# Fused LayerNorm and MLP on one core: two tiles of the first block transposed by DMA, a wave of seven rows, one PSUM ring

## The chip, the core and the metric

The kernel runs on one core of a Trainium2 chip. A core has five engines with instruction queues of their own: TensorE (PE, matrix multiplication; its weight loads are shown as PEld), VectorE (DVE), ScalarE (ACT), GpSimd (POOL) and SyncE (SP, which here only issues DMAs and waits for them). They work side by side and wait for one another through semaphores. PE writes its results to PSUM, which has 8 banks of 512 float32 values on each of 128 partitions; all other data lies in SBUF, also on 128 partitions.

The metric is the device time of one execution in microseconds (us). Lower is better.

## What is computed

```python
def _layernorm(x, axis=-1, eps=1e-5):
    m = jnp.mean(x, axis=axis, keepdims=True)
    v = jnp.var(x, axis=axis, keepdims=True)
    return (x - m) / jnp.sqrt(v + eps)

def reference(x, w1, b1, w2, b2):
    y = _layernorm(x, axis=-1)
    h = _gelu(jnp.einsum("bsd,df->bsf", y, w1) + b1)
    return jnp.einsum("bsf,fd->bsd", h, w2) + b2
```

There are 2048 tokens (one batch), D = 1024, F = 3584, all in bfloat16. The gelu is the tanh approximation.

## The kernel before

**Tiling.** The 2048 tokens are 16 tiles of 128 (one token on each partition) and 4 blocks of 4 tiles. For each block the kernel computes the first product transposed: a *row* r of it is 128 of the 3584 hidden features (28 rows), by 512 tokens. The stationary operand is a 128x128 piece of `w1_sb`, the moving one is `yT_sb`, the normalized block with features on the partitions; 8 matmuls over D make a row (`pe_cell`, L337 to L350, the matmul's line is L344). ACT takes the row out of PSUM with bias and gelu into `hT_sb` (`act_gelu`, L354). The second product then takes `hT_sb` as the stationary operand and `w2_sb` as the moving one: 28 matmuls of 512 columns make one half of an output tile (`out_chunk`, L387), which VectorE adds `b2` to and puts into `o_sb` (L398), and SyncE stores (L403).

**LayerNorm and transposes.** VectorE computes mean and variance of a tile (L252, L256), adds eps (L263), GpSimd takes the power -0.5 (L260), and VectorE normalizes in place in `x_sb` (L268, event `y{i}`). Then the tile has to be transposed into `yT_sb`. For blocks 1 to 3 VectorE does this with 32x32 transposes (L300), in the time that it has left. For block 0 TensorE does it, since everything waits for it: `pe_T` (L311) makes eight 128x128 transposes (L316) into the PSUM tile `ps_t`, and ACT copies them to `yT_sb` in two halves (L324, events `te{i}_0` and `te{i}_1`, for the two halves of D in `KGROUPS`).

**The opening wave.** So that PE can start on tile 0 alone, the first `R` = 4 rows of block 0 are computed tile by tile (L424 to L436), each in its own bank, as *cells* of 128 columns. For each tile, the first half of D is done for all four rows, then the transposes of the next tile are put in, then the second half. With the last tile the four rows go to gelu. The remaining rows of block 0 are whole rows of 512 columns (`mm1_rows(0, R)`). Ahead of the wave, PE runs matmuls on a tile of ones (`warm`, L409), and one small transpose for the bias `b1` (L419).

**Loads.** All loads are issued at the start, without waits, three pieces of x by ACT and the rest by SyncE, each queue in order: parts of tiles 0 to 3, `b1`, and w1 in eight chunks. Chunks 0 to 3 are 256 columns wide with half of D each, chunks 4 and 5 have 512 columns (chunk 4: rows 4 to 7, chunk 5: rows 8 to 11), 6 and 7 have 1024. Then come block 1 of x, w2, b2, and the other blocks of x. A matmul waits for the chunk that its row lies in.

**PSUM.** Three pools: `ps_t` (one bank) for the transposes, `ps_1` with `NB1` = 5 banks for rows of the first product, taken in turn by `new_unit`, and `ps_2` with `NB2` = 2 banks for the halves of output tiles. A bank is taken again when its gelu, or its output addition, has been done.

**Order.** Each engine's instructions are put down as a list in program order; waits are on named events. Only on VectorE the order is planned: `crit` (output additions, with the estimated time at which PE is done) and `fill` (LayerNorm and transposes of the next block) are merged by estimated times (L471 to L486). On PE, ACT, SyncE and GpSimd the order is that of the code.

Of the kernel before, what the change touches and what calls it, by code (L numbers as in the profile page):

```python
# [5 lines left out]
ACT = mybir.ActivationFunctionType  # L6
# [5 lines left out]
P = 128  # L12
TB = 512
TPB = TB // P
R_WAVE = 4
K_GROUPS = 2
NB1 = 5
NB2 = 2
NOB = 2
TAIL_PIECES = 4  # L20
WARM_A = ((26, None), (8, "st0_0"), (8, "mv0"), (6, "rstd0"))
# [63 lines left out]
def bass_standalone__mixer_channel_mlp__prompt_kernel(  # L85
# [18 lines left out]
    HC = D // 2  # L104
    assert ST % TB == 0 and D % P == 0 and F % P == 0 and D % NCH == 0
    assert HC <= 512 and DT * P * 2 <= 2048 and FT >= 4 and FT <= P
    R = max(1, min(R_WAVE, FT - 2, NB1 - 1))
    nkg = max(1, min(K_GROUPS, DT))
    KGROUPS = [(h * DT // nkg, (h + 1) * DT // nkg) for h in range(nkg)]
    assert NB1 + NB2 + 1 <= 8  # L110

    w1_chunks = []
    c0 = 0
# [28 lines left out]
    with ExitStack() as es:  # L142
# [18 lines left out]
        vpe_sb = sb("vpe_sb", [P, NT], F32)  # L161
        rstd_sb = sb("rstd_sb", [P, NT], F32)

        ps_t = ps("ps_t", [P, 1, 1024], BF16)
        ps_1 = ps("ps_1", [P, NB1, 512], F32)
        ps_2 = ps("ps_2", [P, NB2, 512], F32)
        ps_2b = ps_2[:, :, :].bitcast(BF16)

        sp = _Prog(None)
        pe = _Prog("s_pe")  # L170
# [140 lines left out]
        def pe_T(i):  # L311
            waits = [f"y{i}", "ident"]
            if last_te[0] is not None:
                waits.append(last_te[0])
            for j in range(DT):
                pe.op(lambda e, i=i, j=j: e.transpose(out=ps_t[:, 0, j * P:(j + 1) * P],  # L316
                                                      in_=x_sb[:, i, j * P:(j + 1) * P], identity=ident[:, :]),
                      waits=waits if j == 0 else (), sig=(f"tp{i}" if j == DT - 1 else None))
            blk, t = divmod(i, TPB)
            evs = []  # L320
            for h, (j0, j1) in enumerate(KGROUPS):
                src = ps_t[:, 0, j0 * P:j1 * P].rearrange("p (j s) -> p j s", j=j1 - j0)
                dst = yT_sb[:, blk % 2, j0:j1, t * P:(t + 1) * P]
                act.op(lambda e, dst=dst, src=src: e.copy(out=dst, in_=src), waits=[f"tp{i}"], sig=f"te{i}_{h}")  # L324
                evs += [f"te{i}_{h}"] * (j1 - j0)
            yT_ev[i] = evs
            last_te[0] = evs[-1]

        unit_n = [0]
        unit_gelu = []  # L330

        def new_unit():
            u = unit_n[0]
            unit_n[0] += 1
            return u % NB1, ([unit_gelu[u - NB1]] if u >= NB1 else [])

        def pe_cell(b, r, t0, t1, bank, waits, sig, dts=None):  # L337
            n0, n1 = t0 * P, t1 * P
            dts = list(range(DT)) if dts is None else list(dts)
            waits = list(waits)  # L340
            for k, dt in enumerate(dts):
                w = (waits if k == 0 else []) + [f"w1c{w1_chunk_of(r, dt)}"]
                w += [yT_ev[b * TPB + t][dt] for t in range(t0, t1)]
                pe.op(lambda e, b=b, r=r, dt=dt, n0=n0, n1=n1, bank=bank: e.matmul(  # L344
                    ps_1[:, bank, n0:n1], lhsT=w1_sb[:, dt, r * P:(r + 1) * P], rhs=yT_sb[:, b % 2, dt, n0:n1],
                    start=(dt == 0), stop=(dt == DT - 1)),
                    waits=w, sig=(sig if dt == DT - 1 else None))
            pe_t[0] += len(dts) * _mm_us(n1 - n0)
            if dts[-1] == DT - 1:
                est[sig] = pe_t[0]  # L350

        def act_gelu(r, t0, t1, bank, wait_ev, sig):
            n0, n1 = t0 * P, t1 * P
            act.op(lambda e, r=r, n0=n0, n1=n1, bank=bank: e.activation(  # L354
                out=hT_sb[:, r, n0:n1], in_=ps_1[:, bank, n0:n1], func=ACT.Gelu_apprx_tanh,
                bias=b1_sb[:, r:r + 1], scale=1.0),
                waits=[wait_ev, "b1c"], sig=sig)
            unit_gelu.append(sig)

        hT_row = {}  # L360

# [5 lines left out]
            hT_row[(b, r)] = f"g_{b}_{r}"  # L367
            mm1_done[b] = sig

        grp_n = [0]  # L370
        grp_oe = []
        crit = []
        fill = []
        store_last = {}

        def out_chunk(b, st, c0, c1, region, prev_store):
            ti = b * TPB + st
            ob = ti % NOB
            g = grp_n[0]
            grp_n[0] += 1  # L380
            bank = g % NB2
            sig = f"m2_{ti}_{c0}"
            waits = [f"w2c{ci}" for ci in range(nw2c)]
            if g >= NB2:
                waits.append(grp_oe[g - NB2])
            for ft in range(FT):
                pe.op(lambda e, st=st, ft=ft, c0=c0, c1=c1, bank=bank: e.matmul(  # L387
                    ps_2[:, bank, 0:c1 - c0], lhsT=hT_sb[:, ft, st * P:(st + 1) * P], rhs=w2_sb[:, ft, c0:c1],
                    start=(ft == 0), stop=(ft == FT - 1)),
                    waits=(waits if ft == 0 else []) + [hT_row[(b, ft)]],  # L390
                    sig=(sig if ft == FT - 1 else None))
            pe_t[0] += FT * _mm_us(c1 - c0)
            est[sig] = pe_t[0]
            dwaits = [sig, "b2"]
            if prev_store is not None:
                dwaits.append(prev_store)
            oe = f"oe_{ti}_{c0}"
            crit.append((est[sig], (lambda e, ob=ob, c0=c0, c1=c1, bank=bank: e.tensor_tensor(  # L398
                out=o_sb[:, ob, c0:c1], in0=ps_2[:, bank, 0:c1 - c0], in1=b2_sb[:, c0:c1], op=ALU.add),
                dwaits, oe, 0.2 + (c1 - c0) * 1e-3), b))  # L400
            grp_oe.append(oe)
            sev = f"st_{ti}_{c0}"
            sp.op(lambda e, ti=ti, ob=ob, c0=c0, c1=c1: e.dma_start(of[ti * P:(ti + 1) * P, c0:c1], o_sb[:, ob, c0:c1]),  # L403
                  waits=[oe], sig=sev, sem=f"d_st_{ob}_{region}", inc=16)
            store_last[(ob, region)] = sev

        def warm(n, gate=None):
            for _ in range(n):
                pe.op(lambda e: e.matmul(ps_2[:, NB2 - 1, 0:P], lhsT=ones[:, :], rhs=ones[:, :],  # L409
                                         start=True, stop=True), waits=["ones"] + ([gate] if gate else []))  # L410

        act.op(lambda e: e.preload_act_table(ACT.Gelu_apprx_tanh))  # L412
# [2 lines left out]
        for o in ln_seq(list(range(TPB))):  # L415
            dve_put(o)

        pe_T(0)
        pe.op(lambda e: e.transpose(out=ps_2b[:, 0, 0:FT], in_=b1r_sb[:, :], identity=ident[0:FT, 0:FT]),  # L419
              waits=["ident", "b1"], sig="b1t")  # L420
        act.op(lambda e: e.copy(out=b1_sb[:, :], in_=ps_2b[:, 0, 0:FT]), waits=["b1t"], sig="b1c")  # L421
        warm(N_WARM_B)
        wave = [new_unit() for _ in range(R)]
        for t in range(TPB):  # L424
            lastt = (t == TPB - 1)
            for h, (j0, j1) in enumerate(KGROUPS):
                for r in range(R):
                    sig = f"m1_0_{r}" if lastt else f"m1_0_{r}_w{t}"
                    pe_cell(0, r, t, t + 1, wave[r][0], wave[r][1] if (t == 0 and h == 0) else [], sig,
                            dts=range(j0, j1))  # L430
                    if lastt and j1 == DT:
                        act_gelu(r, 0, TPB, wave[r][0], sig, f"g_0_{r}")
                        hT_row[(0, r)] = f"g_0_{r}"
                if t + 1 < TPB and h == 0:
                    pe_T(t + 1)
                    pe_t[0] += DT * 0.056  # L436

        def mm1_rows(b, r0):
            for r in range(r0, FT):
                mm1_row(b, r)  # L440

        mm1_rows(0, R)
        for b in range(NB):
            if b + 1 < NB:
                tiles = list(range((b + 1) * TPB, (b + 2) * TPB))
                rel = est[x_ev[tiles[0]][0]]
                for o in ln_seq(tiles):
                    fill.append((rel, o, b + 1))
                rel_t = max(rel, est[mm1_done[b - 1]] if b - 1 in mm1_done else 0.0)
                for i in tiles:  # L450
                    for o in ops_T(i):
                        fill.append((rel_t, o, b + 1))
            if b > 0:
                mm1_rows(b, 0)
            for st in range(TPB):
                for dh in range(DH):
                    c0, c1 = dh * NCH, (dh + 1) * NCH
                    ob = (b * TPB + st) % NOB
                    prev = store_last.get((ob, dh))
                    last = (b == NB - 1 and st == TPB - 1 and dh == DH - 1)  # L460
                    if last and TAIL_PIECES > 1:
                        pw = NCH // TAIL_PIECES
                        for k in range(TAIL_PIECES):
                            out_chunk(b, st, c0 + k * pw, c0 + (k + 1) * pw, dh if k == 0 else f"{dh}p{k}", prev)
                    else:
                        out_chunk(b, st, c0, c1, dh, prev)

        for sev in store_last.values():
            sp.op(None, waits=[sev])
# [74 lines left out]
```

## Time and profile before

| | us |
|---|---|
| median of 3 runs | 400.81 (400.67 to 400.83) |
| span of the profiled execution, first to last instruction | 399.1 |
| PE, matmuls of the first product (L344), busy | 193.9 |
| PE, matmuls of the second product (L387), busy | 193.2 |
| ACT, gelu (L354), busy | 76.7 |
| VectorE, transposes of blocks 1 to 3 (L300), busy | 83.7 |
| PE, transposes of block 0 (L316), 32 in all, busy | 2.5 |

"Busy" is the union of the times in which an instruction of the group runs. The median is 1.7 us more than the span; the profile shows nothing of what lies around the span. The granted TensorE clock is full in all 40 slices of the page. The DMA engines are at 90% or more for the first six slices, some 55 us, while the weights are loaded, and nearly idle afterwards.

Matmuls overlap in the trace: one of 128 columns is shown with 219 ns, but a new one begins every 56 ns. The chain of waits, which follows one piece of work to the next, is what their pace is read from.

### The profile page before, as it was taken

The page shows a single profiled execution, that of the slowest core. Times are in us where ns is not written, and L with a number is a line of the kernel's source. Part 1 is how long each engine was busy: PE and PEld are TensorE (multiplying, and loading weights), DVE is VectorE, ACT ScalarE, POOL GpSimd, SP SyncE. Part 2 cuts the span into 40 slices and gives each one's busy share as a digit, 9 for nine tenths or more (in the row PEclk, how much of TensorE's full clock was granted, in tenths as well). Part 3 has the DMA queues.
Part 4 walks back from the last instruction along what each step waited for, and adds up shares of the span by engine and source line. Part 5 has one row for each costly group of instructions (what it writes and reads, how often), then busy time and mean ns, then how long its engine had stood idle before and what let it go on. Part 6 is the DMA issues. An engine that isn't in the chain of part 4 may idle for free.

```text
span 399.1 us, 4683 instructions
## 1 busy us (share of the span) xinstructions
PE 393.4 (99%) x2026; PEld 189.5 (47%) x2061; DVE 140.1 (35%) x307; ACT 82.3 (21%) x122; POOL 9.5 (2%) x23
## 2 busy tenths in 40 slices
PE   8999999999999999999999999999999999999997
PEld 7844444444444444444444444444444444444446
DVE  6208999889894004988100000001100000001101
ACT  2544330000044332000024334100003334400000
POOL 1102000100001000000000000000000000000000
PEclk9999999999999999999999999999999999999999
DMA  8999930000000000000000000000000000000001
GB/s 262 370 386 387 387 133 15 26 13 29 26 1 2 0 0 2 26 15 26 27 15 0 0 2 0 6 21 26 15 26 13 2 0 0 2 13 26 15 26 28
DMA packets 17614, 23.64 MB, mean 59 GB/s; under 512 B 1466, under 2 KB 10042, under 8 KB 17594
## 3 DMA queue, kind: packets, MB, share of 16 engines
q1 hardware_dynamic: 17162, 22.95, 16.5%
q10 hardware_dynamic: 432, 0.39, 0.3%
q8 instruction: 16, 0.26, 0.3%
q14 instruction: 4, 0.03, 0.0%
HBM read 19.14 MB, written 4.19 MB: 58 GB/s over the span
## 4 chain that ended last, share of the span: by engine, by line
PE 97%; DMA 1%; DVE 1%; issue 1%; POOL 0%; DVEq 0%
PE ps L344 48%; PE ps L387 48%; DMA x_sb<-in_x_dram 1%; PE ps_t L316 1%; DVE st_sb L252 0%; POOL rstd_sb L260 0%; DVE x_sb L268 0%; PE ps L409 0%; DVE o_sb L398 0%; DVE mv_sb L256 0%; DVE vpe_sb L263 0%; PE ps L419 0%; DVEq L72 0%
## 5 line engine op out<-in xcount | busy, mean ns | idle before, releaser
L344 PE MATMUL ps<-yT_sb,w_sb 128*128 128x512 bf16 (+1 forms) x976 | 193.9, 358 | 0.9
L387 PE MATMUL ps<-w_sb,hT_sb 128*128 128x512 bf16 (+1 forms) x961 | 193.2, 360 | 1.0
L344 PEld LDWEIGHTS ps<-yT_sb,w_sb 128*128 128x128 bf16 x992 | 91.8, 98 | 101.9 <-issue 0.2
L387 PEld LDWEIGHTS ps<-w_sb,hT_sb 128*128 128x128 bf16 x980 | 91.3, 98 | 102.6
L354 ACT ACTIVATE hT_sb<-ps,b_sb 128x512 bf16<-128x512 f32 x112 | 76.7, 688 | 257.2 <-PE ps L344 257.2
L300 DVE STREAM_TRANSPOSE yT_sb<-x_sb 32x256 bf16<-32x256 bf16 x192 | 83.7, 436 | 32.5 <-PE ps L344 29.6
L398 DVE TENSOR_TENSOR o_sb<-ps,b_sb 128x512 bf16<-128x512 f32 (+1 forms) x35 | 22.6, 646 | 198.6 <-PE ps L387 198.4
L252 DVE BATCH_NORM_STATS2 st_sb<-x_sb 128x6 f32<-128x512 bf16 x32 | 21.6, 685 | 20.3 <-DMA x_sb<-in_x_dram 20.3
L260 POOL TENSOR_TENSOR rstd_sb<-vpe_sb,nhalf 128x1 f32<-128x1 f32 x16 | 8.8, 550 | 114.6 <-DVE vpe_sb L263 114.6
L268 DVE TENSOR_SCALAR x_sb<-x_sb,mv_sb,rstd_sb 128x1024 bf16<-128x1024 bf16 x16 | 8.7, 547 | 3.4 <-POOL rstd_sb L260 2.7
L409 PE MATMUL ps<-ones 128*128 128x128 bf16 x56 | 5.6, 276 | 1.4 <-POOL ones L245 1.0
L324 ACT COPY yT_sb<-ps_t 128x512 bf16<-128x512 bf16 x8 | 4.3, 589 | 7.3 <-PE ps_t L316 7.3
L409 PEld LDWEIGHTS ps<-ones 128*128 128x128 bf16 x56 | 4.7, 127 | 2.0 <-POOL ones L245 1.0
L256 DVE BATCH_NORM_AGGREGATE mv_sb<-st_sb 128x2 f32<-128x12 f32 x16 | 3.4, 209 | 1.7
L263 DVE TENSOR_SCALAR vpe_sb<-mv_sb 128x1 f32<-128x1 f32 x16 | 2.5, 154 | 0.6
L316 PE MATMUL ps_t<-ident,x_sb 128*128 128x128 bf16 x32 | 2.5, 220 | 0.1
L316 PEld LDWEIGHTS ps_t<-ident,x_sb 128*128 128x128 bf16 x32 | 1.8, 98 | 0.4 <-DVE x_sb L268 0.2
L412 ACT ACT_TABLE_LOAD x1 | 1.3, 1283 | 2.2 <-issue 2.2
L246 POOL TENSOR_SCALAR_AFFINE_SELECT ident<-ones 128x128 bf16<-128x128 bf16 x1 | 0.3, 294 | 0.1
L245 POOL MEMSET ones<- 128x128 bf16 x1 | 0.2, 205 | 0.3 <-POOLq L529 0.3
L421 ACT CAST b_sb<-ps 128x28 f32<-128x28 bf16 x1 | 0.2, 200 | 0.0
L419 PE MATMUL ps<-ident,b1r_sb 28*128 28x28 bf16 x1 | 0.2, 183 | 0.0
(6 smaller groups left out, 0.6 us busy)
## 6 DMA issues: line engine op xcount, KB each, us to landing
w_sb<-in_w_dram SPq DMA_DIRECT2D x4, 1792.0 KB, 18.4
w_sb<-in_w_dram SPq DMA_DIRECT2D x2, 2048.0 KB, 16.2
out_dram<-o_sb SPq DMA_DIRECT2D x31, 128.0 KB, 1.7
x_sb<-in_x_dram SPq DMA_DIRECT2D x3, 1024.0 KB, 14.1
w_sb<-in_w_dram SPq DMA_DIRECT2D x2, 1024.0 KB, 9.0
w_sb<-in_w_dram SPq DMA_DIRECT2D x4, 256.0 KB, 4.7
x_sb<-in_x_dram SPq DMA_DIRECT2D x2, 256.0 KB, 4.3
x_sb<-in_x_dram ACTq DMA_DIRECT2D x3, 128.0 KB, 3.4
```

The costliest lines, as they stand in the source:

```text
L252: return (lambda e, i=i, h=h: e.bn_stats(st_sb[:, i, 6 * h:6 * (h + 1)], x_sb[:, i, h * HC:(h + 1) * HC]), [x_ev[i][h]], f"st{i}_{h}", 0.65)
L256: return (lambda e, i=i: e.bn_aggr(mv_sb[:, i, :], st_sb[:, i, :]), [f"st{i}_0", f"st{i}_1"], f"mv{i}", 0.33)
L260: pool.op(lambda e, i=i: e.tensor_tensor(out=rstd_sb[:, i:i + 1], in0=vpe_sb[:, i:i + 1], in1=nhalf[:, i:i + 1], op=ALU.pow), waits=[f"vpe ...
L268: return (lambda e, i=i: e.tensor_scalar(out=x_sb[:, i, :], in0=x_sb[:, i, :], scalar1=mv_sb[:, i, 0:1], scalar2=rstd_sb[:, i:i + 1], op0= ...
L300: res.append((lambda e, src=src, dst=dst: e.transpose(out=dst, in_=src), waits, (f"tr{i}" if lastop else None), 0.47))
L316: pe.op(lambda e, i=i, j=j: e.transpose(out=ps_t[:, 0, j * P:(j + 1) * P], in_=x_sb[:, i, j * P:(j + 1) * P], identity=ident[:, :]), waits ...
L324: act.op(lambda e, dst=dst, src=src: e.copy(out=dst, in_=src), waits=[f"tp{i}"], sig=f"te{i}_{h}")
L344: pe.op(lambda e, b=b, r=r, dt=dt, n0=n0, n1=n1, bank=bank: e.matmul(ps_1[:, bank, n0:n1], lhsT=w1_sb[:, dt, r * P:(r + 1) * P], rhs=yT_sb ...
L354: act.op(lambda e, r=r, n0=n0, n1=n1, bank=bank: e.activation(out=hT_sb[:, r, n0:n1], in_=ps_1[:, bank, n0:n1], func=ACT.Gelu_apprx_tanh, ...
L387: pe.op(lambda e, st=st, ft=ft, c0=c0, c1=c1, bank=bank: e.matmul(ps_2[:, bank, 0:c1 - c0], lhsT=hT_sb[:, ft, st * P:(st + 1) * P], rhs=w2 ...
L398: crit.append((est[sig], (lambda e, ob=ob, c0=c0, c1=c1, bank=bank: e.tensor_tensor(out=o_sb[:, ob, c0:c1], in0=ps_2[:, bank, 0:c1 - c0], ...
L409: pe.op(lambda e: e.matmul(ps_2[:, NB2 - 1, 0:P], lhsT=ones[:, :], rhs=ones[:, :], start=True, stop=True), waits=["ones"] + ([gate] if gat ...
```

## The change

In block 0, only tiles 0 and 1 are still transposed by `pe_T` (`N_PE_T` = 2). For tiles 2 and 3 ACT issues a DMA that transposes from `x_sb` to `yT_sb` (`act_T`), after the tile has been normalized. The wave has seven rows (`R` + `R_LATE`). PE first does four rows on tiles 0 and 1 as before; then rows 4 to 6 on both tiles together, as 256 columns; then all seven rows on tile 2, and on tile 3, in cells of 128 columns and over the whole of D. After the wave come rows 7 to 27.

The three PSUM pools become one of eight banks, `ps_a`, through which rows and output halves go in turn (`new_unit`, with `bank_free` holding the event that frees a bank). Bank 7 is used for the transposes of tiles 0 and 1 and is the eighth unit, so row 7 waits for the copies of tile 1. The warming matmuls and the small transpose of `b1` write to banks 5 and 6.

On PE, 16 transposes fall away; rows 4 to 6 of block 0 are 24 matmuls of 256 and 48 of 128 columns in place of 24 of 512. On ACT, four copies fall away and two DMAs are added. On VectorE, the plan comes out slightly different: one output addition stands ahead of a normalization instead of behind it, and the transposes around block 0's first output additions are 52, 11 and 1 in place of 53 and 11. The order on SyncE and GpSimd is the same.

```diff
 R_WAVE = 4
+R_LATE = 3
+N_PE_T = 2
-NB1 = 5
-NB2 = 2
+NBANK = 8
+WARM_BANK = 5
+B1_BANK = 6
+T_BANK = 7
...
-        ps_t = ps("ps_t", [P, 1, 1024], BF16)
-        ps_1 = ps("ps_1", [P, NB1, 512], F32)
-        ps_2 = ps("ps_2", [P, NB2, 512], F32)
-        ps_2b = ps_2[:, :, :].bitcast(BF16)
+        ps_a = ps("ps_a", [P, NBANK, 512], F32)
+        ps_ab = ps_a[:, :, :].bitcast(BF16)
...
+        def act_T(i):
+            blk, t = divmod(i, TPB)
+            dst = yT_sb[:, blk % 2, :, t * P:(t + 1) * P]
+            act.op(lambda e, i=i, dst=dst: e.dma_start_transpose(dst, x_sb[:, i, :]), waits=[f"y{i}"], sig=f"dt{i}",
+                   sem=f"d_dt{i}", inc=16)
+            yT_ev[i] = [f"dt{i}"] * DT
...
         def new_unit():
             u = unit_n[0]
             unit_n[0] += 1
-            return u % NB1, ([unit_gelu[u - NB1]] if u >= NB1 else [])
+            bank = u % NBANK
+            return bank, ([bank_free[bank]] if bank in bank_free else [])
...
-        wave = [new_unit() for _ in range(R)]
-        for t in range(TPB):
-            lastt = (t == TPB - 1)
+        wave = [new_unit() for _ in range(RW)]
+        bank_free[T_BANK] = f"te{N_PE_T - 1}_{len(KGROUPS) - 1}"
+        for t in range(N_PE_T):
             for h, (j0, j1) in enumerate(KGROUPS):
                 for r in range(R):
-                    sig = f"m1_0_{r}" if lastt else f"m1_0_{r}_w{t}"
-                    pe_cell(0, r, t, t + 1, wave[r][0], wave[r][1] if (t == 0 and h == 0) else [], sig,
+                    pe_cell(0, r, t, t + 1, wave[r][0], wave[r][1] if (t == 0 and h == 0) else [], f"m1_0_{r}_w{t}",
                             dts=range(j0, j1))
-                    if lastt and j1 == DT:
-                        act_gelu(r, 0, TPB, wave[r][0], sig, f"g_0_{r}")
-                        hT_row[(0, r)] = f"g_0_{r}"
-                if t + 1 < TPB and h == 0:
+                if t + 1 < N_PE_T and h == 0:
                     pe_T(t + 1)
                     pe_t[0] += DT * 0.056
+        for t in range(N_PE_T, TPB):
+            act_T(t)
+        for r in range(R, RW):
+            waits = ["b1c"] if r == B1_BANK else ([])
+            pe_cell(0, r, 0, N_PE_T, wave[r][0], waits, f"m1_0_{r}_w0")
+        for t in range(N_PE_T, TPB):
+            lastt = (t == TPB - 1)
+            for r in range(RW):
+                sig = f"m1_0_{r}" if lastt else f"m1_0_{r}_w{t}"
+                pe_cell(0, r, t, t + 1, wave[r][0], [], sig)
+                if lastt:
+                    act_gelu(r, 0, TPB, wave[r][0], sig, f"g_0_{r}")
+                    hT_row[(0, r)] = f"g_0_{r}"
...
-        mm1_rows(0, R)
+        mm1_rows(0, RW)
```

## The prediction

> **What bounds the kernel now.** I read the page's busy times first, then the chain of waits, then the opening of that chain in order of time. The first lines are from the page.
>
> ```profile
> span 399.1 us, 4683 instructions
> ...
> PE 393.4 (99%) x2026; PEld 189.5 (47%) x2061; DVE 140.1 (35%) x307; ACT 82.3 (21%) x122; POOL 9.5 (2%) x23
> ...
> PE 97%; DMA 1%; DVE 1%; issue 1%; POOL 0%; DVEq 0%
> ```
>
> TensorE (PE) holds 97% of the chain that ends last. So a change counts in two ways only: it takes matmul time off, or it makes PE wait. The stretch that is changed lies in the first 22 us. The chain there (start us, us, engine and line, count) is:
>
> ```profile
> 8.93 0.50 PE ps_t L316 x8
> 9.42 1.79 PE ps L344 x32
> 11.21 0.52 PE ps_t L316 x8
> 11.73 1.79 PE ps L344 x32
> 13.52 0.53 PE ps_t L316 x8
> 14.05 2.68 PE ps L344 x48
> 16.73 0.05 issue
> 16.78 10.74 PE ps L344 x49
> ```
>
> The reader is to see that PE already runs through: transposes of tiles 1, 2, 3 (L316) between cells of the wave (L344), with no DMA or ACT piece among them. Out of it come three prices. A 128-column cell matmul takes 1.79/32 = 0.0559 us. A 512-column one takes (10.74 + 0.05)/49 = 0.2202 us. The two tiles whose transposes go took 0.52 + 0.53 us. Rows 4 to 6 (24 matmuls of 512 columns from 16.78) end at 16.78 + 24 x 0.2202 = 22.07. At that point the same work is done before and after the change: the first product of block 0 for rows 0 to 6. I compare there, and nothing later differs on PE.
>
> Two inputs set what the new order can do. VectorE's timeline has the normalized tiles 1, 2 and 3:
>
> ```profile
> 8.20 0.55 DVE L268 TENSOR_SCALAR x_sb<-x_sb,mv_sb,rstd_sb 128x1024 bf16<-128x1024 bf16 x1
> ...
> 10.51 0.55 DVE L268 TENSOR_SCALAR x_sb<-x_sb,mv_sb,rstd_sb 128x1024 bf16<-128x1024 bf16 x1
> ...
> 12.82 0.55 DVE L268 TENSOR_SCALAR x_sb<-x_sb,mv_sb,rstd_sb 128x1024 bf16<-128x1024 bf16 x1 [0.67 <-POOL rstd_sb L260]
> ```
>
> Tile 2 is ready at 11.06, tile 3 at 13.37. Second, the loads on SyncE's queue. Its timeline gives the issue (start us, us), and the DMA view of that one issue, in the fence after it, the us from issue to landing (last number):
>
> ```profile
> 5.43 0.43 SPq L183 DMA_DIRECT2D w_sb<-in_w_dram  x1
> ```
>
> ```profile
> w_sb<-in_w_dram SPq DMA_DIRECT2D x1, 1024.0 KB, 7.2
> ```
>
> This is w1 chunk 4, the columns of rows 4 to 7: it lands at 5.43 + 7.2 = 12.63. Before, nobody noticed, since row 4 starts at 16.78.
>
> **The change, part by part.** *Removed from PE:* 16 transposes, 0.52 + 0.53 = 1.05 us, all on the chain. Their four ACT copies (589 ns each in the page's groups) go too; ACT had idle time around them, so nothing. *Regrouped:* rows 4 to 6 become 24 matmuls of 256 columns and 48 of 128 columns. No row shows 256 columns; between the two prices per 128 columns (0.0559 and 0.2202/4 = 0.0551) it is 0.110 to 0.112, I take 0.111: 24 x 0.111 = 2.66, and 48 x 0.0559 = 2.68, sum 5.34 against 5.29, so +0.05. The issue gap of 0.05 I leave out on the new side. Were nothing late, the new order would run: 48 cells from 9.42 (tile 0's second half and tile 1) to 12.10, late rows over tiles 0 and 1 to 14.76, then 56 cells of tile 2 (3.13) and 56 of tile 3 (3.13) to 21.02. That is 1.05 us before 22.07.
>
> *New wait 1, weights.* The late rows' first cell needs chunk 4, which lands at 12.63, not 12.10. From a release to the first result the chain needs 0.18 us (tile 1 ready 8.75, first transpose 8.93). So they begin at 12.81: 0.71 us of the 1.05 are gone, the late rows end at 15.47, and the floor for the whole is 15.47 + 6.26 = 21.73, which is -0.34. Behind this wait stands all of PE's queue, that is everything.
>
> *New wait 2, tile 2 by DMA.* ACT's queue now waits for tile 2 after the copies of tile 1 (9.46 + 1.07 = 10.53 in its timeline, so it is there in time), and issues at about 11.11. Behind it on ACT stand the second DMA and the gelus, the first of which is not due before tile 3's cells; they lose nothing. PE wants the tile for 15.47, so 4.2 us from issue are free, and each us more costs one us. *New wait 3, tile 3:* issued at 13.42, wanted at 18.60 less 0.18, so 5.0 us are free. The trace has no DMA transpose. The nearest rows are loads of the same 256 KB tile, those of tiles 2 and 3 on SyncE:
>
> ```profile
> x_sb<-in_x_dram SPq DMA_DIRECT2D x1, 256.0 KB, 3.2
> ```
>
> ```profile
> x_sb<-in_x_dram SPq DMA_DIRECT2D x1, 256.0 KB, 5.4
> ```
>
> The first met short queues, the second stood behind 1 MB of weights in its own queue. The transpose has ACT's queue to itself but meets weights on the same 16 engines (the windows from 8 to 14 us give a full DMA share, at 347 to 352 GB/s). ACT's last 128 KB load, in that position, took 3.4 us; 128 KB more at half of 350 GB/s are 0.75, so I take 3.4 + 0.8 = 4.2. Then tile 2 lands at 15.31, its cells start at 15.49 and the end is 21.75: -0.32. Tile 3 lands at 17.62 and doesn't count. With 3.2 the floor holds (-0.34); with 5.4 tile 2 lands at 16.51, the end is 16.51 + 0.18 + 6.26 = 22.95, +0.88. The far bound is a DMA with as many runs: in the diff its destination is 8 pieces of 128 elements on each of 128 partitions, 1024 pieces, as many as the 1 MB chunks have (8 pieces of 512 on 128 partitions). Those took 7.2 (chunk 4) and 10.8 (chunk 5, the next issue). They are rival 1.
>
> A rule that speaks against the change: the Trainium skill, "VectorE: DVE Perf Modes", section "The three transpose paths", puts one 128x128 block at 390 ns on TensorE and 1309 ns by DMA, and advises TensorE where the result may go to PSUM. The trace has TensorE at 0.5 us for eight blocks, far below eight times 390. Eight DMA blocks one after the other would be an estimated 10.5 us a tile; tile 3 would land near 32 us, and the kernel would need some 414 us. Against that stands "Advanced Engine Details and Errata", section "X-Bar Transpose (TRN2)": transposing DMAs are as fast as others. By this the sum would be the one above. No row here shows either.
>
> *Moved and paid nowhere.* The 0.5 MB of transpose traffic takes about 1.5 us from the loads at 350 GB/s. Chunk 5 (issued 5.91, landing 16.7) is wanted by row 8, after 21.7 + 1.8 = 23.5: 6.8 us of cover. SyncE's order of DMAs stays; POOL's too. *One PSUM ring:* a bank comes back after eight units instead of five (rows) or two (output groups); its release was a gelu (688 ns) or an eviction (646 ns) with at least one unit of 1.76 us between, and PE's whole idle time on these lines is 1.9 us. Nothing is gained or lost; without cover it would cost some 0.7 us a group. VectorE moves one eviction ahead of a normalization and splits its transposes 52 and 12 instead of 53 and 11; those are 0.4 us of an engine with 35% load, whose first block-0 eviction waits for PE. Nothing.
>
> **The sum.** -1.05 + 0.05 - 0.05 + 0.71 + 0.02 = -0.32 us: a span of 398.8 in place of 399.1. The median of the runs, 400.81, is 1.7 above the span; carried over, 400.5 us. What can be told from no change here is about 0.2%, 0.8 us, so this is no change.
>
> **The rivals.** *1, slower: the DMAs move piece by piece.* If 1024 short pieces take turns with the weights' rows, a tile costs what a 1024-row chunk costs. With 7.2 us tile 2 lands at 18.31 and the end is 24.75: +2.7, 403.5 us. With 10.8 for tile 3, which follows in the same queue, 13.42 + 10.8 + 0.18 + 3.13 = 27.5: +5.5, 406.3. It decides from a landing 5.3 us after issue (+0.8). For it: the engines are saturated until 55 us. Against: bytes are a quarter of a chunk's. *2, slower: ACT's issue is held.* SyncE's own issues get stuck once much is queued, as its timeline shows:
>
> ```profile
> 9.92 2.92 SPq L183 DMA_DIRECT2D w_sb<-in_w_dram  x1
> ...
> 12.88 5.43 SPq L183 DMA_DIRECT2D x_sb<-in_x_dram  x1
> ```
>
> If what holds them is shared by both queues, tile 3's DMA starts at 18.36 and lands at 22.56; the end is 25.87: +3.8, 404.6. Against: ACT's three issues took 0.46 us each, but before the queues were full. *3, faster: chunk 4 is in time.* Were its last part early enough, the end would be 21.02: -1.05, 399.8 us. Against: this needs it 0.7 us earlier and tile 2 within 3.5 us, and the new traffic can only delay it.
>
> **How the numbers follow.** Forecast 0.50, of which 0.06 over +0.8 (the 5.4 row); its own range is 400.3 to 401.7. Rival 1 0.22, rival 2 0.18, rival 3 0.08, and 0.02 for smaller losses over 0.8. Faster by over 0.2%: 0.08. Within: 0.44. Slower: 0.06 + 0.22 + 0.18 + 0.02 = 0.48. Losses have more cases, each smaller than the forecast. The range leaves out rival 3 below and rival 1's upper half above: 400.2 to 404.7.
>
> **What would show it.** Right: the chain has a DMA piece of w_sb of about 0.5 us ahead of the 256-column matmuls, both transposes land within 4 to 5 us of issue, and row 7 starts near 21.7 us. Rival 1: the DMA view gives the transposes over 5.3 us and PE's wait names yT_sb. Rival 2: ACT's issue itself lasts us. Rival 3: no piece for w_sb. The forecast is wrong if PE's idle time in the first 25 us exceeds 1.5 us, or if the rest of the kernel no longer runs at 0.2202 us a matmul.

## The result and the profile after

The changed kernel needs 411.56 us (411.50 to 411.68, 4 runs) against 400.82 us of the kernel before in the same session (400.67 to 400.92): a ratio of 1.0266, 95% interval 1.0254 to 1.0278. That is slower by 10.7 us. The profiled execution agrees: a span of 409.9 us in place of 399.1.

The page of the changed kernel, part 4 (the chain that ended last, by engine and by line), has a new entry: the DMA transpose.

```profile
PE 92%; DMA 5%; SPq 1%; DVE 1%; issue 1%; POOL 0%; DVEq 0%
PE ps_a L406 47%; PE ps_a L355 45%; DMA yT_sb<-x_sb 4%; DMA x_sb<-in_x_dram 1%; SPq L186 1%; DVE st_sb L255 0%; DVE x_sb L271 0%; POOL rstd_sb L263 0%; DVE o_sb L391 0%; DVE mv_sb L259 0%; DVE vpe_sb L266 0%; DVEq L76 0%
```

Its timeline in the opening (start us, us, engine, line; in brackets the idle time before and what ended it):

```profile
11.22 8.15 ACTq L335 DMA_TRANSPOSE yT_sb<-x_sb  x2
...
13.04 2.79 PE L355 MATMUL ps_a<-yT_sb,w_sb 128*128 128x256 bf16 x24 [0.80 <-DMA w_sb<-in_w_dram]
...
23.20 5.89 PEld L355 LDWEIGHTS ps_a<-yT_sb,w_sb 128*128 128x128 bf16 x56 [7.65 <-DMA yT_sb<-x_sb]
23.20 6.08 PE L355 MATMUL ps_a<-yT_sb,w_sb 128*128 128x128 bf16 x56 [7.37 <-DMA yT_sb<-x_sb]
```

PE waits 0.8 us for chunk 4, runs the late rows, and then stands still for 7.4 us for tile 2. Then the 56 cells of tile 2 take 6.08 us; those of tile 3 take 3.30 in the chain below. The DMA view of the two transposes, one issue at a time (last number: us from issue to landing):

```profile
yT_sb<-x_sb ACTq DMA_TRANSPOSE x1, 11.9
```

```profile
yT_sb<-x_sb ACTq DMA_TRANSPOSE x1, 15.9
```

Tile 2 lands at 11.22 + 11.9 = 23.1, tile 3 at 13.53 + 15.9 = 29.4. The chain in order of time shows which of them sets the end:

```profile
13.53 15.89 DMA yT_sb<-x_sb
29.42 0.05 issue
29.47 3.30 PE ps_a L355 x56
32.77 0.05 issue
```

Row 7 starts at 32.82 in place of 22.07: 10.75 us later, which is the whole difference of 10.8 us between the spans. From there on the two kernels run alike.

Why the transposes are slow is seen in the DMA view of the changed kernel for 17 to 21 us (queue: packets, MB, share of 16 engines; q1 is SyncE's queue, q10 ACT's):

```profile
q1 hardware_dynamic: 687, 1.41, 90.2%
q10 hardware_dynamic: 683, 0.17, 19.2%
```

Both queues get the same number of packets, not the same bytes. A packet of the weights has 2048 bytes and takes 0.902 x 16 x 4 us / 687 = 84 ns of an engine; one of a transpose has 256 bytes and takes 18 ns. A closer look, from 18.000 to 18.094 us, shows the turns:

```profile
q1 hardware_dynamic: 16, 0.03, 89.4%
q10 hardware_dynamic: 16, 0.00, 19.1%
```

In 94 ns there are 16 packets of each queue. One of the weights fills 84 ns of an engine, so none of the 16 engines can have two: each takes one packet from each queue in turn. The next four such stretches, to 18.47 us, read the same (80 and 80 in all). A tile is 1024 transpose packets, 64 for each engine. By the packets' times it needs 64 x (84 + 18) = 6.5 us while the weights flow; by these turns, in which the packets overlap a little (the shares add up to 109%), 64 x 0.094 = 6.0. Tile 3 landed 6.3 us after tile 2. And for the first 4 us there are no transpose packets at all (same view, 11.2 to 15.2 us):

```profile
q1 hardware_dynamic: 1308, 1.41, 107.9%
q8 instruction: 1, 0.02, 1.8%
```

### The profile page after: what moved, and what is told of

It is laid out like the page before. It is cut to its first block, busy times and chain, and to the rows that moved or that the text cites. A ratio compares the mean times of both kernels' runs of the same rounds, so it can differ in the third digit from the quotient of the medians.

```text
span 409.9 us, 4744 instructions
## 1 busy us (share of the span) xinstructions
PE 395.7 (97%) x2058; PEld 194.0 (47%) x2093; DVE 140.1 (34%) x307; ACT 79.8 (19%) x118; POOL 9.6 (2%) x23
## 3 DMA queue, kind: packets, MB, share of 16 engines
q1 hardware_dynamic: 17162, 22.95, 16.2%
## 4 chain that ended last, share of the span: by engine, by line
PE 92%; DMA 5%; SPq 1%; DVE 1%; issue 1%; POOL 0%; DVEq 0%
PE ps_a L406 47%; PE ps_a L355 45%; DMA yT_sb<-x_sb 4%; DMA x_sb<-in_x_dram 1%; SPq L186 1%; DVE st_sb L255 0%; DVE x_sb L271 0%; POOL rstd_sb L263 0%; DVE o_sb L391 0%; DVE mv_sb L259 0%; DVE vpe_sb L266 0%; DVEq L76 0%
## 5 line engine op out<-in xcount | busy, mean ns | idle before, releaser
L355 PE MATMUL ps_a<-yT_sb,w_sb 128*128 128x512 bf16 (+2 forms) x1021 | 196.9, 354 | 9.5 <-DMA yT_sb<-x_sb 7.6
L406 PE MATMUL ps_a<-w_sb,hT_sb 128*128 128x512 bf16 (+1 forms) x964 | 193.4, 360 | 0.8
L355 PEld LDWEIGHTS ps_a<-yT_sb,w_sb 128*128 128x128 bf16 x1040 | 97.0, 101 | 108.4 <-DMA yT_sb<-x_sb 8.0
L406 PEld LDWEIGHTS ps_a<-w_sb,hT_sb 128*128 128x128 bf16 x980 | 91.3, 98 | 102.6
L365 ACT ACTIVATE hT_sb<-ps_a,b_sb 128x512 bf16<-128x512 f32 x112 | 76.3, 688 | 272.8 <-PE ps_a L355 272.8
L391 DVE TENSOR_TENSOR o_sb<-ps_a,b_sb 128x512 bf16<-128x512 f32 (+1 forms) x35 | 22.6, 646 | 208.4 <-PE ps_a L406 208.3
L255 DVE BATCH_NORM_STATS2 st_sb<-x_sb 128x6 f32<-128x512 bf16 x32 | 21.6, 685 | 21.9 <-DMA x_sb<-in_x_dram 21.8
L417 PE MATMUL ps_a<-ones 128*128 128x128 bf16 x56 | 5.6, 276 | 1.5 <-POOL ones L248 1.0
L417 PEld LDWEIGHTS ps_a<-ones 128*128 128x128 bf16 x56 | 4.7, 127 | 2.1 <-POOL ones L248 1.0
L327 ACT COPY yT_sb<-ps_a 128x512 bf16<-128x512 bf16 x4 | 2.1, 589 | 5.0 <-PE ps_a L319 5.0
L319 PE MATMUL ps_a<-ident,x_sb 128*128 128x128 bf16 x16 | 1.2, 220 | 0.1
```

The source lines that it names most:

```text
L255: return (lambda e, i=i, h=h: e.bn_stats(st_sb[:, i, 6 * h:6 * (h + 1)], x_sb[:, i, h * HC:(h + 1) * HC]), [x_ev[i][h]], f"st{i}_{h}", 0.65)
L417: pe.op(lambda e: e.matmul(ps_a[:, WARM_BANK, 0:P], lhsT=ones[:, :], rhs=ones[:, :], start=True, stop=True), waits=["ones"] + ([gate] if g ...
```

## The experiments

All are edits of the changed kernel. Ratios are against the kernel before, measured in the same session (400.85 to 400.94 us).

**e1_hold_loads.** Are the transposes slow by themselves, or by company?

```diff
+        sp.op(None, waits=[f"dt{TPB - 1}"])
         for ci in range(len(w1_chunks)):
             if ci not in w1_issued:
                 load_w1(ci)
```

> SyncE waits for both transposes before it issues w1 chunk 5 and all later loads, so the transposes meet no weights. Theory A (in the changed kernel each 256-byte packet of a transpose takes turns with one 2048-byte packet of the weights, 84 + 18 ns a pair and engine, 64 pairs a tile): tile 2 lands within 6 us of its issue in place of 11.9, tile 3 within 6 in place of 15.9, and the kernel needs 401 to 403 us. Theory B (the transpose itself is slow, whatever else the engines do): tile 2 again lands about 12 us after issue, tile 3 about 6 us later, and the time stays at 411 to 413. Theory C, on the 4.1 us between issue and the first packet (11.22 to 15.3): if ACT's issue is held up by SyncE's queued loads, the first packet comes 1 to 1.5 us after issue here; if the transpose's own preparation takes it, 4 us stay.

Measured: 401.28 us (400.55 to 401.67), ratio 1.0007 (0.9997 to 1.0016). The DMA view of tile 2's and tile 3's transpose, and the queues from 14 to 16.2 us:

```profile
yT_sb<-x_sb ACTq DMA_TRANSPOSE x1, 4.1
```

```profile
yT_sb<-x_sb ACTq DMA_TRANSPOSE x1, 3.1
```

```profile
q10 hardware_dynamic: 1581, 0.39, 89.4%
```

Alone, the same transposes land in 4.1 and 3.1 us, at 0.39 MB in 2.2 us = 177 GB/s, and the loss is gone. The first packet comes 1.2 us after issue. So theory B falls and A holds. C was still open: both a stuck issue and packets lying ahead are gone here.

**e2_short_packets.** The same bytes of weights in packets of 512 bytes.

```diff
-W1_CHUNK_COLS = (256, 256, 512, 512, 1024, 1024)
+W1_CHUNK_COLS = (256, 256, 512) + (256,) * 10
```

> All weights after chunk 4 are loaded in chunks of 256 columns, so their packets have 512 bytes (27 ns each in the opening) in place of 1024 and 2048; the bytes are the same. Theory A (turns packet by packet): 64 pairs of 27 + 18 ns are 2.9 us a tile in place of 6.5; tile 2 lands at 18 to 20 us, tile 3 about 3 us later, the kernel needs 404 to 407 us. If the engines share by bytes or the transpose is limited by itself, the landings stay at 23 and 29 us and the time at 411 to 412.

Measured: 406.43 us (405.25 to 407.57), ratio 1.0139 (1.0119 to 1.0158). The DMA view of the two transposes:

```profile
yT_sb<-x_sb ACTq DMA_TRANSPOSE x1, 8.0
```

```profile
yT_sb<-x_sb ACTq DMA_TRANSPOSE x1, 10.0
```

They landed at 19.1 and 23.4 us, against 23.1 and 29.4. The size of somebody else's packets sets their pace; the bytes had not changed. The turns were less regular here: 1069 packets of transposes to 879 of weights from 14.6 to 18.5 us, with a pause in it (see the last section).

**e3_keep_pe_busy.** What did the clock cost? The windows of the changed kernel show it halved (us, busy PE, PEld, DVE, ACT, POOL, then granted clock, DMA share, GB/s):

```profile
18.00:20.00 2.00, 0.00 (x0) 0.00 (x0) 0.00 (x0) 0.00 (x0) 0.00 (x0) 0.71 1.07 387
20.00:22.00 2.00, 0.00 (x0) 0.00 (x0) 0.00 (x0) 0.00 (x0) 0.00 (x0) 0.50 1.09 379
...
26.00:28.00 2.00, 2.00 (x22) 2.00 (x20) 0.00 (x0) 0.00 (x0) 0.00 (x0) 0.50 1.09 393
```

```diff
+        for _ in range(132):
+            pe.op(lambda e: e.matmul(ps_a[:, T_BANK, 0:P], lhsT=ones[:, :], rhs=ones[:, :],
+                                     start=True, stop=True), waits=["ones", f"te{N_PE_T - 1}_{len(KGROUPS) - 1}"])
         for t in range(N_PE_T, TPB):
             lastt = (t == TPB - 1)
```

> 132 matmuls on the tile of ones (56 ns each, results unused, in the bank of row 7 before row 7 takes it) fill PE's wait for tile 2. Theory: the halved clock from 18.8 to 29 us costs nothing, since the slow cells of tile 2 end at 29.3 us when tile 3 lands at 29.4; with a full clock PE waits for tile 3 instead, and the time changes by less than 0.5 us from 411.6. Rival: the clock is part of the loss, and the time falls by up to 2.9 us, to 408.7.

Measured: 414.51 us (412.91 to 415.53), ratio 1.0337 (1.0316 to 1.0357): 3 us more, which neither side expected. The clock stayed full, and PE's timeline reads:

```profile
24.45 3.30 PE L355 MATMUL ps_a<-yT_sb,w_sb 128*128 128x128 bf16 x56 [1.70 <-DMA yT_sb<-x_sb]
30.70 3.30 PE L355 MATMUL ps_a<-yT_sb,w_sb 128*128 128x128 bf16 x56 [2.95 <-DMA yT_sb<-x_sb]
```

In this execution, the fastest (412.91 us), the part on the clock holds: tile 2's cells now take 3.3 us, and PE waits 2.95 us for tile 3 instead, which sets the end in both kernels. But both tiles landed 1.2 to 1.3 us later than in the changed kernel (24.4 and 30.7): the transfers nearly stopped from about 21.6 to 22.8 us, soon after a 16 KB instruction packet at 21.0 (kind "instruction" in the DMA view). The changed kernel has no such packet between 14.1 and 30.8; the added matmuls seem to have brought it. The other three executions have no timeline; their mean clock is 0.992 to 0.996, so in them it did fall for a while, and the rest of their 3 us is not explained.

**e4_tiles_by_pe.** The new order and the ring, without DMA transposes.

```diff
-        bank_free[T_BANK] = f"te{N_PE_T - 1}_{len(KGROUPS) - 1}"
+        bank_free[T_BANK] = f"te{TPB - 1}_{len(KGROUPS) - 1}"
...
-        for t in range(N_PE_T, TPB):
-            act_T(t)
+        pe_T(2)
         for r in range(R, RW):
...
             for r in range(RW):
+                if r == 0 and not lastt:
+                    pe_T(t + 1)
```

> The new order and the PSUM ring stay, but tiles 2 and 3 are transposed by PE again, tile 2 ahead of the late rows, tile 3 ahead of tile 2's cells. If the DMA transposes are the whole loss, the time is 400.7 to 401.3 us (0.53 + 0.50 for the transposes back, 0.05 for the split rows, 0.2 for the weights: about +0.2 against before). If ring or wave cost something of their own, it stays over 402.

Measured: 401.06 us (400.88 to 401.46), ratio 1.0006 (0.9998 to 1.0015). The wave and the one PSUM ring cost nothing that can be told; the DMA transposes are the whole loss.

**e5_hold_and_fetch_earlier.** Does an instruction packet on one engine hold up a transpose?

```diff
+        sp.op(None, waits=[f"dt{TPB - 1}"])
...
-        for n, gate in WARM_A:
-            warm(n, gate)
+        for _ in range(2 * WARM_A[0][0]):
+            pe.op(lambda e: e.matmul(ps_a[0:64, WARM_BANK, 0:64], lhsT=ones[:, 0:64], rhs=ones[:, 0:64],
+                                     start=True, stop=True), waits=["ones"])
+        for n, gate in WARM_A[1:]:
+            warm(n, gate)
```

> As e1_hold_loads, and the first group of 26 warming matmuls of 128 columns is 52 of 64 columns with 64 weight columns, so that the 16 KB instruction fetch that e1's trace shows at 12.20 us (1.08 us long, on one DMA engine) comes some 26 matmuls earlier, near 10.7, before the first transpose packet at 12.25. Theory D (the pause of all transpose packets in e1, 13.1 to 14.0, is the other 15 engines waiting for the one that fetches): the pause is gone, tile 2 lands 3.0 to 3.3 us after issue in place of 4.1, and the time is 400.3 to 400.7 us with less spread than e1's 400.55 to 401.67. Theory E (the first transpose pauses by itself, some 0.7 us after its first packet, as in the changed kernel, where no fetch lay near): the pause stays and tile 2 again takes about 4 us.

Measured: 401.32 us (400.27 to 403.83), ratio 1.0010 (0.9996 to 1.0024). In the profiled execution the packet came at 11.9, not 10.7, but ended at 13.0, just as the first transpose packet came; the pause was gone and tile 2 landed 3.1 us after issue. The packet had moved by 0.3 us only; the transposes came 0.7 us later too, issued at 11.80 in place of 11.12. The time didn't follow: there PE waited 0.47 and 0.97 us for weights, which landed later than in e1. It fits theory D and settles nothing on the time.

**e6_hold_two_chunks.** Where do the first 4 us go?

```diff
             if ci not in w1_issued:
+                if ci == 7:
+                    sp.op(None, waits=[f"dt{TPB - 1}"])
                 load_w1(ci)
```

> SyncE waits for both transposes only before w1 chunk 7 (the second of 1024 columns), so chunks 5 and 6 lie queued on the engines when ACT issues at 11.1, but SyncE is not stuck in an issue. Theory S (the 4.1 us to the first packet come from SyncE's stuck issue): first packet about 1.2 us after issue, as in e1, tile 2 lands at 18 to 19 us, tile 3 at 20 to 21, the kernel needs about 404 us. Theory Q (packets already queued on the engines go first): first packet again 3.5 to 4.5 us after issue, near 15, tile 2 lands at 19.5 to 21, tile 3 one or two us later, the kernel needs 405 to 406.

Measured: 411.15 us (409.50 to 411.33), ratio 1.0247 (1.0232 to 1.0261). SyncE's last issue ended at 9.8 us, and at 11.18, when ACT issued, it did nothing but wait. Yet the DMA view from 11.2 to 15.2 us again has no packet of ACT's queue:

```profile
q1 hardware_dynamic: 1290, 1.40, 108.3%
q8 instruction: 1, 0.02, 1.7%
```

So theory S falls. What is already queued goes first: 1290 packets are 81 for each engine; the 1.2 us that pass in e1 too are about 24 of them, so some 57 packets lay ahead. Where they wait, on the DMA engines or ahead of them, the trace doesn't show. The time was underestimated: chunks 5 and 6, slowed by the turns themselves, lasted until 21.5 us, and tile 2 landed at 22.8 with the clock at half.

**e7_hold_small_chunk, e8_small_chunk_and_fetch.** Chunk 4 cut to the columns of rows 4 to 6.

```diff
-W1_CHUNK_COLS = (256, 256, 512, 512, 1024, 1024)
+W1_CHUNK_COLS = (256, 256, 384, 128, 512, 1024, 1024)
...
+                if ci == 6:
+                    sp.op(None, waits=[f"dt{TPB - 1}"])
```

> As e1_hold_loads, but chunk 4 holds only the 384 columns of rows 4 to 6, row 7's 128 columns follow as a chunk of their own, then SyncE waits for the transposes. Theory: chunk 4 lands about 0.7 us earlier (256 KB less at 350 GB/s), near 11.9, so PE's wait for the weights (0.72 us in e1) goes; tile 2, which lands about 15.2, is then the limit (wanted 14.6): the end of rows 0 to 6 moves from 21.9 in e1 to 21.2 to 21.6, and the time is 399.9 to 400.9 us.

> Both edits, of e5 and e7. By theory D tile 2 lands near 14.3, in time, and rows 0 to 6 end near 21.05: 1.0 us before the kernel before, 399.8 to 400.1 us. By theory E it equals e7.

Measured: e7 400.63 us (400.44 to 400.84), ratio 0.9993 (0.9985 to 1.0002); e8 400.68 us (400.48 to 401.39), ratio 0.9997 (0.9988 to 1.0005). In e7's timeline the wait for weights is gone, and tile 2 is next, as expected:

```profile
15.31 18.95 PE L357 MATMUL ps_a<-yT_sb,w_sb 128*128 128x128 bf16 x168 [0.44 <-DMA yT_sb<-x_sb]
```

In e8 the instruction packet stayed at 12.4 us, so its edit didn't do what it was for, and D was not tested there; that e8 equals e7 is what theory E had forecast.

**e9_hold_eight_rows, e10_syncE_transposes.** Cover for that wait, and then the other queue. Both keep e7's chunks, and e9 its hold.

```diff
-R_LATE = 3
+R_LATE = 4
...
-            waits = ["b1c"] if r == B1_BANK else ([])
+            waits = {B1_BANK: ["b1c"], T_BANK: [bank_free[T_BANK]]}.get(r, [])
```

e10 has no hold; instead

```diff
+        def sp_T(i):
+            dst = yT_sb[:, 0, :, i * P:(i + 1) * P]
+            sp.op(lambda e, i=i, dst=dst: e.dma_start_transpose(dst, x_sb[:, i, :]), waits=[f"y{i}"], sig=f"dt{i}",
+                  sem=f"d_dt{i}", inc=16)
...
+                if ci == 6:
+                    for t in range(N_PE_T, TPB):
+                        sp_T(t)
                 load_w1(ci)
...
-        for t in range(N_PE_T, TPB):
-            act_T(t)
```

> As e7_hold_small_chunk, with row 7 as a fourth late row (its bank is the one of the transposes, free since tile 1's copies). The late rows over tiles 0 and 1 then take 32 x 0.111 = 3.55 us from 12.10 to 15.65, so tile 2 (15.3 in e7) is in time and PE's last wait in the opening is gone. Theory: rows 0 to 7 end at 15.65 + 128 x 0.0559 = 22.8, against 22.07 + 1.76 = 23.83 in the kernel before: 1.0 us less, 399.7 to 400.1 us. Rival: the opening transposes that were taken off PE come back as another wait (tile 3, or row 8's weights, which land near 21.5), and the time stays at 400.4 to 400.9.

> As e9, but SyncE issues both transposes in its own queue between row 7's weights and chunk 6, so nothing waits for their landing; later loads queue behind them. If a transpose takes turns only with other queues' packets, tile 2 lands 3.1 to 4.2 us after its issue at 11.1 and tile 3 3 to 5 us after 13.4, although loads follow at once, and the time equals e9's within 0.3 us. If the loads behind still get in between, tile 3 lands after 19 and the time is over 401.

Measured: e9 400.44 us (400.11 to 400.73), ratio 0.9988 (0.9979 to 0.9997); e10 400.19 us (400.10 to 400.85), ratio 0.9983 (0.9974 to 0.9992). e9's rival was right, in time and cause: row 8's weights came late, since chunk 6 waited for the landing. In e10 that is gone too. PE's timeline of e9, then of e10:

```profile
23.34 10.95 PE L357 MATMUL ps_a<-yT_sb,w_sb 128*128 128x512 bf16 x50 [0.41 <-DMA w_sb<-in_w_dram]
```

```profile
9.39 24.88 PE L364 MATMUL ps_a<-yT_sb,w_sb 128*128 128x128 bf16 x260
```

From tile 1's transposes on, PE in e10 has no wait left. The transposes landed 4.2 and 3.1 us after issue although 1 MB and more of weights was issued right behind them, in the same queue, from 14.82 us on. The DMA view from 14.3 to 16.2 us has hardly anything but transpose packets:

```profile
DMA packets 1596, 0.40 MB, mean 213 GB/s; under 512 B 1580, under 2 KB 1596, under 8 KB 1596
```

So e10 shows that the transposes and the loads behind them hardly met. SyncE's wait for tile 3 held those loads back as well, so how the two would fare side by side in one queue is not shown.

**e12_eight_rows_by_pe.** Is e10's gain the transposes? Chunks and eight rows of e10, tiles 2 and 3 by PE:

```diff
-        for t in range(N_PE_T, TPB):
-            act_T(t)
-        for r in range(R, RW):
+        pe_T(2)
+        for r in range(R, RW - 1):
...
+            if not lastt:
+                pe_T(t + 1)
+                bank_free[T_BANK] = f"te{t + 1}_{len(KGROUPS) - 1}"
             for r in range(RW):
+                if r == RW - 1 and not lastt:
+                    pe_cell(0, r, 0, N_PE_T, wave[r][0], [bank_free[T_BANK]], f"m1_0_{r}_w0")
```

> The control for e10: the same chunks and eight rows, but tiles 2 and 3 are transposed by PE, ahead of the late rows and of tile 2's cells, and the loads run on without a break. If e10's gain is the 16 transposes taken off PE, this needs 1.0 us more than e10: 401.0 to 401.3. If the chunks or the wave made the gain, it equals e10's 400.2.

Measured: 400.98 us (400.73 to 401.39), ratio 1.0003 (0.9994 to 1.0012), 0.8 us over e10. The gain is that of the transposes taken off PE. For the smallest mend, the changed kernel with seven rows and nothing but the queue exchanged (e11_only_the_queue, expected at 400.4 to 401.2 us), there is no result, so what the queue alone is worth is not shown.

## Why the prediction was wrong

- **What is saved on PE: right.** 1.05 us was the bound; e10 reaches 0.75 us, and e12 without the DMA transposes reaches nothing.
- **Wait for chunk 4: right.** The landing was forecast at 12.63 and the first late cell at 12.81; it came at 13.04, with the opening itself 0.13 late; 0.8 us of wait against 0.71.
- **Regrouped rows, ring, VectorE's order: right.** e4 stands at 1.0006 (0.9998 to 1.0015).
- **The landing of tile 2: wrong, and this step decides.** It took "128 KB more at half of 350 GB/s", that is, it let the two queues share the engines by bytes, and got 4.2 us. Measured: 11.9. Some 4.2 us pass before the first packet, 7 with turns, packet by packet (64 for each engine at 94 to 102 ns, and a pause of some 0.7), and 0.7 from the last packet to the landing. Taken alone the number was right by luck of the row: 4.1 us in e1, with no weights about.
- **The landing of tile 3: wrong twice.** 4.2 us were counted from its own issue. It stands behind tile 2 in ACT's queue, and its 64 turns start when tile 2's are over: it landed at 29.4, 6.3 us after tile 2. Tile 3, which "doesn't count", ends the wait.
- **Rival 1 was what happened, priced too low.** Its 7.2 and 10.8 came from chunks whose packets have 1024 bytes and take turns with nobody. Its far end, +5.5, had tile 3's place behind tile 2, by the row of chunk 5 behind chunk 4, but not the 4 us of queued packets and the 2048 bytes of the partner's packets: 15.9 us in place of 10.8. Hence a range that ended at 404.7. (That the engines are full until 55 us is a little long: the page's DMA line has 8, 9, 9, 9, 9 and 3 tenths in the first six slices, which is some 53 us. Nothing hangs on it.)
- **Rival 2's sign came, but not its cost.** ACT's second issue did last 5.84 us, 13.53 to 19.37, against 1.26 in e1. With SyncE idle, in e6, it lasted 5.66, with the same 4 us before tile 2's first packet, so SyncE's stuck issue is not what held it. And it was over before tile 2 had landed (23.1), behind which tile 3 stood in any case.
- **The clock was not in the working at all.** It fell to half some 3 us into the wait and cost 2.8 us of cells (6.08 against 3.30), all of it hidden behind tile 3's landing (e3). In e6, where tile 3 lands soon after tile 2, it shows: 112 cells take 7.74 us, against 6.43 in e7. The Trainium skill, "TensorE: Matmul & The Clock Gate", Part 1, says that an idle window of about 3.4 us halves the clock. The trace is near that: PE's last matmul ended at 15.83, and the 0.71 of the window from 18 to 20 us puts the fall at 18.8, which is 3.0 us.

A rule of the skill bears on the failed step: "DMA: Bandwidth & Descriptors", "Queues, rings and completion order", lets an engine take turns between queues at packet granularity, with some 9 to 17 descriptors to a packet. The trace agrees on turns and, if each of its records is a descriptor, differs on their size: one 256-byte record for one of 2048 bytes, 683 to 687 in 4 us and 16 to 16 in 94 ns. And the 1309 ns a block of "VectorE: DVE Perf Modes", "The three transpose paths", are no price for a tile: eight blocks landed in 3.1 to 4.1 us in e1, not in the 10.5 estimated from it. That transposing DMAs are as fast as others ("Advanced Engine Details and Errata", "X-Bar Transpose (TRN2)") is not so here either: 177 GB/s alone in e1 and 213 in e10's view, where loads have 346 to 388.

## What to carry to other kernels

A DMA of many short packets, put on a queue of its own beside a bulk load, got here one short packet for each long one, and first waited for what was already queued: price it by its packets times the partner's packet time, not by its bytes. Issue it in the queue of the bulk load, ahead of the loads that it must not meet: in e10, which also has the cut chunk and an eighth row, 11.9 us became 4.2, and the loss of 10.7 us a gain of 0.75. Two such transfers in one queue followed each other, so the second one's landing is the one to compute.

## What the runs showed of the hardware

A transpose seems to need all 16 DMA engines in step. In e1 a 16 KB instruction packet lay on one engine from 12.2 to 13.3 us, and the DMA view from 13.2 to 14.0 us shows what followed:

```profile
DMA packets 27, 0.01 MB, mean 9 GB/s; under 512 B 27, under 2 KB 27, under 8 KB 27
```

27 packets in 0.8 us, with 8.2% of the time of 16 engines, are about one engine's work. It looks as if the late engine works off its share while 15 stand still. The changed kernel paused as well, from 16.3 to 16.9 us, some 0.8 us after its first transpose packets. The view from 16.30 to 16.85 us:

```profile
q1 hardware_dynamic: 6, 0.01, 5.8%
q10 hardware_dynamic: 4, 0.00, 0.8%
```

Together that is 6.6% of 16 engines, one engine at work, and the other engines' weights stand still with their transposes. But no instruction packet lay near: the last had ended at 14.0, 1.4 us before the first transpose packet. So why an engine would be late there is open, and theory E, a pause by itself soon after the first packets, fits this pause as well as e1's. For theory D speak e5, where no pause came, with the packet over before the first transpose packet, and e3, where a second one came 6 us after the first packets, with a second instruction packet. That the instruction packet is the cause is an inference from these places; no run moved the packet and nothing else.
